# r1 and u of a chunked recurrence as products of 128 rows and 80 columns, decay trees on other engines, and 38 unread products

## The chip, the core and the metric

One core of a Trainium2 chip. The metric is the device time of one execution in microseconds (us), the median of three runs. TensorE is called PE, VectorE DVE, ScalarE ACT, GpSimd POOL, and SP is the queue of SyncE that issues most DMAs.

## What is computed

An RWKV-7 recurrence over four batches, eight heads and 768 steps, with a state of 40x40 for each head, followed by a layer of eight experts that a hash of the token's id chooses:

```python
for t in range(S):
    y[:, :, t] = np.einsum('bhd,bhde->bhe', rt, state)
    Sa = np.einsum('bhde,bhe->bhd', state, at)
    state_decay = state * wt[:, :, None, :] - np.einsum('bhd,bhe->bhde', Sa, bt)
    state = state_decay + np.einsum('bhd,bhe->bhde', vt, kt)
...
expert_idx = token_ids * np.int64(2654435761) % np.int64(E)
...
    h = np.maximum(xe @ w1[e], 0.0)
    out[mask] = h @ w2[e]
```

The experts have D = 320 and F = 1024, there are 3072 tokens, and everything is fp32.

## The kernel before

**Tiles.** The sequence is cut into chunks of 64 steps. A tile is one chunk of two batches (128 rows, all eight heads), so there are 24 tiles, numbered u = 0 to 23; even and odd ones belong to the two pairs of batches. Within a chunk the recurrence is a triangular system. Its right side is r = A·state + (masked A·k)·v, its solution is u. The inverse is built on DVE for four tiles at once (`group_i`: a transpose `nb`, 31 elimination steps on `ub`, two transposes `ut` and `ug`) and completed on PE as `x` and `um`.

**Decays.** `decays(ri)` serves four tiles: from w it makes a tree `lv` of products over 32 rows, then a tree `p` and a tree `q`, and DVE transposes them to `pt` and `qt`, which multiply a and b into `at` and `be` on POOL (DVE for the first `be`). `p` and `q` share one buffer, and both go to DRAM and come back as `py` and `ql`.

**Order.** Every step is entered in a list with a tick, and the sorted list is the order on PE, DVE, ACT and POOL. Each engine runs its instructions in that order. Tile u has its main tick at u + 8. In a tick PE runs: `r0` (state's share of r, 128 rows by 80 columns), `r1` (share of v), `y0` and `y1` (outputs of the tile before), `u`, `ab`, `um`, `tu`, `sd`, `kv`, `s`, `rc`, `rt`, `ak`, `x` and the transposes `at_t`, `bt`. ACT moves r from PSUM as `rhs`, once a tick, so those copies mark the ticks in a trace; they stand at 73.37 for tile 0 and 412 us or so for tile 22. The experts follow from about 431 us on. SP issues the loads in one order too, and each load that needs a buffer back waits there, with all that is queued behind it.

**r1 and u** are each 16 products of 64 rows, 64 columns of weights and 40 columns of data, in an order (`banked`) that puts four beside one another in the array's quadrants. An fp32 product is two records in the trace, so r1 is 32 records and u is 32. Buffers that hold zeros between heads are cleared once at the start by POOL (L135).

Of the kernel before, what the change touches and what calls it, by code (L numbers as in the profile page):

```python
# [42 lines left out]
def kernel(  # L43
# [113 lines left out]

    z_r = ring("z", 3, [ZW], z_gaps)
    r_r = ring("r", 2, [1, H * C], pair_gaps)
    x_r = ring("x", 3, [2, H * C], pair_gaps)  # L160
# [112 lines left out]
    @at_tick(6.08, order=9)  # L273
# [35 lines left out]
    def decays(ri, times, t_out):  # L309
# [36 lines left out]
        for i in range(4, -1, -1):  # L346
            @step
            def _(i=i):
# [3 lines left out]
                eng = nc.gpsimd if ri in (2,) else nc.vector  # L352
# [10 lines left out]
        for i in range(4, -1, -1):  # L363
            @step
            def _(i=i):
                src = x["w"][:] if i == 0 else lv(i)
                d = 1 << i
                if i == 4:
                    x["q"] = spare(ri) if ri < 2 else early.tile([P, BLK, D], F32, tag="pq", name="q")
                    (nc.vector if ri in () else nc.gpsimd).tensor_copy(x["q"][:, BLK - 1], x["ends"][:])  # L370
                q = x["q"]
                eng = nc.vector if ri in () else nc.gpsimd
# [41 lines left out]
    def turned(x, tick, step, src, dst, bufs, by=lambda hp: ident[:]):  # L414
# [18 lines left out]
    def stage_a(u):  # L433
# [4 lines left out]
        if u < 3 * GRP:  # L438
            m = 4.45 + 0.37 * (u - GRP) if u < 2 * GRP else 10.3 + 0.2 * (u - 2 * GRP)
            return m, m + 0.29, m + 0.37  # L440
        return u - 1.4 + (1.0 if u == 3 * GRP else -0.1 if u == 3 * GRP + 1 else 0), None, None

    def tile_a(u):
# [15 lines left out]
        def _():  # L459
# [6 lines left out]
            eng = nc.vector if u < 2 else nc.gpsimd  # L466
# [18 lines left out]
        else:  # L485
            turned(x, u - 1, "at", lambda hp: x["at"][:, hp, :], "at_t", LAG + 2, turning)
# [4 lines left out]
        def _():  # L491
            x["ab_ps"] = p = psum("ab_ps")
            for hp in range(HP):
                for blk in range(2):
                    for par in range(2):
                        for hf in range(2):
                            t0 = blk * BLK
                            r0 = kept(hp, hf) * C + (BLK - t0 if swapped(hp) else t0)
                            o = p[r0:r0 + BLK, par, hp * C:(hp + 1) * C]
                            lhs = x["bt"][half(par), hp, hf, t0:t0 + BLK]  # L500
                            rhs = x["at_t"][half(par), hp, hf, :]
                            if swapped(hp):

                                rhs = bass.AP(rhs.tensor, rhs.offset + BLK, [rhs.ap[0], (-BLK, 2), (1, BLK)])
                            else:
                                rhs = rhs.rearrange("p (two t) -> p two t", two=2)
                            if blk:
                                rhs = rhs[:, 1].unsqueeze(1).to_broadcast([C, 2, BLK])
                            mm(o.rearrange("p (two t) -> p two t", two=2), lhs, rhs)

        @(at_tick(u, "ab", after=0.0) if t_ab is None else at_tick(t_ab + 0.01))
        def _():
# [4 lines left out]
            nc.scalar.copy(groups[gi]["ab"][:, ti].rearrange("p (two h) t -> p two (h t)", two=2), p[:, :, 0:HP * C])  # L517
# [53 lines left out]
    if 0:  # L571
        warm(7.78 - 0.01, 0, gate=True)
    for t_, n_ in ():
        warm(t_, n_)

    def tile_m(u, t0):
# [10 lines left out]
        @(at_tick(t0 - 2, "x") if u > 1 else at_tick(7.78 + 0.02 * u))  # L587
# [10 lines left out]
        @(at_tick(t0 - 2, "x", after=0.0) if u > 1 else at_tick(7.78 + 0.01 + 0.02 * u))  # L598
# [11 lines left out]
        @(at_tick(t0 - 1, "um") if u else at_tick(7.78 + 0.04))  # L610
# [8 lines left out]
        @(at_tick(t0 - 1, "um", after=0.0) if u else at_tick(7.78 + 0.05))  # L619
# [8 lines left out]
    def tile_s(u, t0):  # L628
# [15 lines left out]
        def _():  # L644
            x["r"], x["x"] = r_r(u), x_r(u)
# [6 lines left out]
        def _():  # L652
            load(lambda hf, rows: x["r"][rows, 0].rearrange("t (h x) -> t h x", x=C)[:, :, 0:D], r, n, g)
# [6 lines left out]
        @(at_tick(t0 - 1.41, order=6) if u != 1 else at_tick(8.21))  # L660
# [6 lines left out]
        @(at_tick(t0 - 1.41 + (0.16 if u > 3 else 0.0), order=6) if u != 1 else at_tick(8.21))  # L667
# [40 lines left out]
        turned(x, t0 - 1, "rt", lambda hp: x["r"][:, 0, hp * P:hp * P + R], "r_t", 3)  # L708
# [7 lines left out]
    def tile_b(u, t0):  # L716
# [15 lines left out]
        def _():  # L732
            x["r_ps"] = p = psum("r_ps")
            if n:
                for i in range(HQ):
                    for hf in range(2):
                        for bk in range(2):
                            hp = bk * HQ + i
                            mm(p[half(kept(hp, hf)), bk, i * 2 * D:(i + 1) * 2 * D], x["at_t"][0:R, hp, hf, :],
                               heads(st[0:R, hf ^ j, hp, :]), start=i == 0, stop=False)  # L740

        def own(p, s_, hp, par):
            c0 = (hp % HQ * 2 + par) * D
            return p[half(s_), hp // HQ, c0:c0 + D]
# [12 lines left out]

        @at_tick(t0, "u")
        def _():
            x["u_ps"] = p = psum("u_ps")  # L760
            for hp, hf, par in banked():
                s_ = half(kept(hp, hf))
                mm(own(p, hf, hp, par), x["um"][s_, hx(par, hp), :], x["rhs"][s_, of_head(hp, par)])

        @at_tick(t0, "u", after=0.0)
        def _():
            p = x.pop("u_ps")
            for hf in range(2):
                nc.scalar.copy(x["x"][half(hf), hf].rearrange("t (two h x) -> t two h x", two=2, x=C)[:, :, :, 0:D],
                               p[half(hf), :, 0:HQ * 2 * D].rearrange("t two (h x) -> t two h x", x=D))  # L770
# [654 lines left out]
```

## Time and profile before

| | us |
|---|---|
| median of three runs (684.29 to 688.72) | 684.83 |
| profiled execution, device time | 686.91 |
| its span | 685.1 |
| outside the span | 1.81 |
| ticks of the recurrence, first `rhs` to the last | 73 to 422 |
| experts | 431 to 685 |

PE is busy for 85% of the span. The timeline gives each run of equal instructions with its start, its length, and in brackets how long the engine stood idle before it and whom it waited for. The view by stretches gives busy times with the granted clock of PE (1.00 is the higher of its two levels, 0.50 the lower).

### The profile page before, as it was taken

What the parts mean: (1) busy time and instruction counts of PE and PEld (TensorE: products, weight loads), DVE (VectorE), ACT (ScalarE), POOL (GpSimd) and SP (SyncE); (2) the same over time, 40 slices, a digit from 0 to 9 for tenths busy, and PEclk for the clock granted to TensorE, in tenths of its full rate; (3) what the DMA queues carried; (4) which work ended last, traced back from release to release, by engine and by line L of the source; (5) the groups of instructions that cost most, each with busy time, mean ns of one, the idle gap of its engine ahead of it and who ended that gap; (6) DMA issues with size and microseconds to landing.
All of it is one profiled execution on the core that took longest, in us unless ns stands there. A gap on an engine that the chain in (4) does not pass through costs nothing.

```text
span 685.1 us, 25689 instructions
## 1 busy us (share of the span) xinstructions
PE 584.3 (85%) x11337; PEld 451.4 (66%) x11337; DVE 354.4 (52%) x728; ACT 228.2 (33%) x518; POOL 261.4 (38%) x373
## 2 busy tenths in 40 slices
PE   0444888788979888988879899989999999999994
PEld 0333877677868777877768787867656656565662
DVE  8979998387847695663885761211313131311100
ACT  0233444435645456556444444011111111111110
POOL 6344456455653466444434443222113031211111
PEclk9976667769999899999998999999999999999998
DMA  4566666556556657655677742117646535151000
GB/s 109 134 169 123 131 134 165 113 152 139 110 120 172 131 102 187 127 116 120 149 178 185 192 84 53 41 38 240 189 143 213 172 110 163 47 172 39 29 11 23
DMA packets 184873, 86.07 MB, mean 126 GB/s; under 512 B 159066, under 2 KB 176499, under 8 KB 184756
## 3 DMA queue, kind: packets, MB, share of 16 engines
q1 hardware_dynamic: 177972, 71.54, 42.9%
q0 software_dynamic: 6528, 12.17, 5.9%
q8 instruction: 90, 1.47, 0.9%
q10 hardware_dynamic: 256, 0.66, 0.3%
q14 instruction: 27, 0.22, 0.1%
HBM read 68.51 MB, written 16.11 MB: 124 GB/s over the span
## 4 chain that ended last, share of the span: by engine, by line
PE 60%; DVE 11%; issue 8%; POOL 7%; DMA 6%; SPq 3%; ACT 3%; POOLq 0%; DVEq 0%; ACTq 0%
PE up_ps L233 16%; PE dn_ps L233 12%; PE y_ps L233 4%; PE r_ps L233 3%; PE sd_ps L870 3%; SPq L291 3%; PE rc_ps L233 3%; PE s_ps L233 3%; DVE ub L548 2%; DVE outer L546 2%; PE ue_ps L233 2%; PE kv_ps L431 2%; DVE qt L357 2%; DMA bl<-in_b_dram 2%; PE u_ps L233 1%
## 5 line engine op out<-in xcount | busy, mean ns | idle before, releaser
L233 PE MATMUL up_ps<-xt,w 128*128 128x416 f32 (+3 forms) x384 | 110.1, 498 | 1.3 <-DVE xt L1256 1.3
L233 PE MATMUL dn_ps<-w,ht 128*128 128x320 f32 x352 | 97.2, 432 | 0.0
L233 PEld LDWEIGHTS up_ps<-xt,w 128*128 128x128 f32 (+1 forms) x384 | 58.3, 188 | 51.2 <-issue 45.7
L233 PEld LDWEIGHTS dn_ps<-w,ht 128*128 128x128 f32 x352 | 66.3, 190 | 27.6 <-issue 1.1
L1206 DVE TENSOR_SCALAR ht<-up_ps 128x416 f32<-128x416 f32 (+1 forms) x32 | 17.9, 558 | 106.5 <-PE up_ps L233 106.5
L548 DVE TENSOR_TENSOR ub<-ub,outer 128x60 f32<-128x60 f32 (+9 forms) x180 | 63.8, 354 | 6.2
L546 DVE TENSOR_TENSOR outer<-ub,nb 128x60 f32<-128x60 f32 (+9 forms) x180 | 61.5, 342 | 4.2
L1162 POOL DMA_INDIRECT out_dram<-o,tabs x24 | 23.8, 991 | 91.8 <-ACT o L1212 91.8
L855 POOL TENSOR_TENSOR ys<-ys,py 128x320 f32<-128x320 f32 x24 | 20.7, 862 | 73.0 <-ACT ys L850 73.0
L1208 ACT ACTIVATE ht<-up_ps 128x416 f32<-128x416 f32 (+1 forms) x32 | 15.7, 491 | 86.5 <-PE up_ps L233 86.5
L1212 ACT COPY o<-dn_ps 128x320 f32<-128x320 f32 x22 | 9.4, 426 | 99.4 <-PE dn_ps L233 90.4
L1192 DVE COPY xt<-xg_ps 128x384 f32<-128x384 f32 x22 | 11.0, 551 | 58.5 <-PE xg_ps L1191 58.5
L665 POOL TENSOR_TENSOR z<-kb,ql 128x320 f32<-128x320 f32 x24 | 20.8, 868 | 51.7 <-DMA ql<-q_rows 29.0
L799 DVE TENSOR_TENSOR mr<-rc_ps,after_s 128x1024 f32<-128x1024 f32 x24 | 29.3, 1219 | 15.7 <-PE rc_ps L233 15.7
L233 PE MATMUL rc_ps<-r_t,vu 64*64 64x64 f32 x1536 | 31.3, 234 | 2.1 <-issue 1.3
L1291 POOL COPY htq<-ht 128x256 f32<-128x256 f32 x8 | 3.1, 394 | 77.8 <-DVE ht L1206 67.8
L233 PE MATMUL ab_ps<-at_t,bt 64*32 64x64 f32 x1536 | 23.8, 237 | 10.6 <-ACT at_t L484 5.5
L480 PE MATMUL ab_t_ps<-ident,be 128*128 128x128 f32 x48 | 11.5, 380 | 23.5 <-POOL be L467 12.9
L233 PE MATMUL s_ps<-x,z 128*64 128x40 f32 x704 | 30.6, 252 | 0.7 <-issue 0.7
L870 PE MATMUL sd_ps<-ident,st 128*128 128x128 f32 x176 | 29.8, 319 | 1.2 <-issue 1.1
L607 POOL TENSOR_SCALAR um<-ug,first 128x128 f32<-128x128 f32 x48 | 28.4, 597 | 6.3 <-DVE ug L559 6.3
L233 PEld LDWEIGHTS rc_ps<-r_t,vu 64*64 64x64 f32 x1536 | 27.5, 146 | 4.1 <-issue 2.2
(233 smaller groups left out, 1162.6 us busy)
## 6 DMA issues: line engine op xcount, KB each, us to landing
w<-in_moe_w_dram SPq DMA_DIRECT2D x8, 1280.0 KB
w<-in_moe_w_dram SPq DMA_DIRECT2D x8, 1024.0 KB
ql<-q_rows SPq DMA_DIRECT2D x48, 160.0 KB
al<-in_a_dram SPq DMA_DIRECT2D x48, 80.0 KB
bl<-in_b_dram SPq DMA_DIRECT2D x48, 80.0 KB
p_rows<-pt SPq DMA_DIRECT2D x6, 640.0 KB
q_rows<-qt SPq DMA_DIRECT2D x6, 640.0 KB
kb<-in_b_dram SPq DMA_DIRECT2D x48, 80.0 KB
```

The lines of the kernel that those rows point to most:

```text
L233: nc.tensor.matmul(out_, lhsT=lhsT, rhs=rhs, start=start, stop=stop, skip_group_check=True)
L291: nc.sync.dma_start(dst(hf, half(1 - hf if crossed else hf)), src[batch(g, hf, n % 2), :, n * C:(n + 1) * C, :].rearrange("h t e -> t h e"))
L546: nc.vector.tensor_tensor(tv, ub[:, 0:j + 1, j:j + 1].to_broadcast([P, j + 1, m]), nb[:, j, j + 1:].unsqueeze(1).to_broadcast([P, j + 1, m ...
L548: nc.vector.tensor_tensor(o, o, tv, op=OP.add)
L607: nc.gpsimd.tensor_scalar(um[:, i::2, 0:BLK], groups[gi]["ug"][:, ti * H + i:(ti + 1) * H:2, :], first[:, i:i + 1], None, op0=OP.mult)
L665: nc.gpsimd.tensor_tensor(heads(zv), pairs(x["kb"][:, hf]), pairs(x["ql"][:, hf]), op=OP.mult)
L799: nc.vector.tensor_tensor(t[:].rearrange("p two f h t -> p (two f h) t"), x.pop("rc_ps")[:].rearrange("p two (h t) -> p (two h) t", t=C), ...
L855: nc.gpsimd.tensor_tensor(ys[:], ys[:], x["py"][:], op=OP.mult)
L870: nc.tensor.transpose(p[0:R, f, hp * R:(hp + 1) * R], st[0:R, f, hp, :], ident[0:R, 0:R])
L1162: st = nc.gpsimd.indirect_dma_start(out=out[:], out_offset=bass.IndirectOffsetOnAxis(ap=idx, axis=0), in_=o, in_offset=None, bounds_check= ...
L1206: nc.vector.tensor_scalar(ht[:, f, c:end], ps_[f][:], 0.0, None, op0=OP.max)
L1208: nc.scalar.activation(ht[:, f, c:end], ps_[f][:], AF.Relu)
```

## The change

**r1 and u** become eight products each, of 128 rows, 64 columns of weights and 80 columns of data (two heads side by side, written to two places of the output by a stride): 16 records for 32, two beside one another. One half of each operand is zero: `rhs` becomes one buffer of 128x640 that is cleared once, ACT writes its two halves with two copies (64x320 each) where one of 128x320 was, and the half of `x` that u overwrites is cleared again in every tick on POOL (two clearings of 64x320, after the copies of `um` and ahead of `ys`). At the start POOL clears six more pieces of 64x512 and one of 128x640.

**Decay trees.** `lv` of ri = 2 and `p` of ri = 3, 4 and 5 go from DVE to POOL, `q` of ri = 3 from POOL to DVE, and `be` of tile 1 from DVE to POOL. Many ticks shift by 0.01 to 0.2.

**Unread products.** `warm` puts 38 products of 128x128 with 256 columns into PSUM where nobody reads them: ten ahead of the first x, the others in the next five ticks. One more of two columns reads `go`, which DVE writes near the end of the first elimination (62.65 us before).

```diff
-    x_r = ring("x", 3, [2, H * C], pair_gaps)
+    x_r = ring("x", 3, [2, H * C], lambda t: pair_gaps(t) + [t[half(i), i] for i in range(2)])
+    rhs_r = ring("rhs", 1, [HP, 2, 2, D], lambda t: [t])
...
-                (nc.gpsimd if ri in () else nc.vector).tensor_tensor(lv(i), src[:, 0::2], src[:, 1::2], op=OP.mult)
+                (nc.gpsimd if ri in (2,) else nc.vector).tensor_tensor(lv(i), src[:, 0::2], src[:, 1::2], op=OP.mult)
...
-                eng = nc.gpsimd if ri in (2,) else nc.vector
+                eng = nc.gpsimd if ri in (2, 3, 4, 5) else nc.vector
...
-                eng = nc.vector if ri in () else nc.gpsimd
+                eng = nc.vector if ri in (3,) else nc.gpsimd
...
-            eng = nc.vector if u < 2 else nc.gpsimd
+            eng = nc.vector if u < 1 else nc.gpsimd
...
-    if 0:
-        warm(7.78 - 0.01, 0, gate=True)
-    for t_, n_ in ():
+    if 10:
+        warm(7.77 - 0.01, 10, gate=True)
+    for t_, n_ in ([7.97, 3], [8.21, 2], [8.66, 1], [9.02, 4], [9.33, 5], [9.8, 2], [10.34, 4], [10.55, 2], [11.54, 4], [12.08, 1]):
         warm(t_, n_)
...
-            for hp, hf, par in banked():
-                mm(own(p, kept(hp, hf), hp, par), x["mk"][half(1 - hf), par, hp, :],
-                   x["x"][half(1 - hf), hf, wide(hp, par)], start=n == 0 and hp % HQ == 0 and par == 0)
+            for i in range(HQ):
+                for par in range(2):
+                    for s_ in range(2):
+                        hp, other = HQ * s_ + i, HQ * (1 - s_) + i
+                        at0, at1 = wide(hp, par).start, H * C + wide(other, par).start
+                        mm(both(p[half(s_)], (i * 2 + par) * D, HP * D), x["mk"][:, par, hp, :],
+                           both(x["x"].rearrange("p f c -> p (f c)"), at0, at1 - at0),
+                           start=n == 0 and i == 0 and par == 0)
...
-            nc.scalar.copy(rhs[:].rearrange("p (two x) -> p two x", two=2), x.pop("r_ps")[:, :, 0:HQ * 2 * D])
+            for s_ in range(2):
+
+                o = rhs[half(s_)]
+                o = bass.AP(o.tensor, o.offset + s_ * D, [o.ap[0], (HP * 2 * D + D - 2 * D * s_, 2), (2 * D, HP), (1, D)])
+                nc.scalar.copy(o, p[half(s_), 0:HP * 2 * D].rearrange("p (f h e) -> p f h e", f=2, e=D))
...
-            for hp, hf, par in banked():
-                s_ = half(kept(hp, hf))
-                mm(own(p, hf, hp, par), x["um"][s_, hx(par, hp), :], x["rhs"][s_, of_head(hp, par)])
+            for i in range(HQ):
+                for par in range(2):
                     for hf in range(2):
+                        mm(both(p[half(hf)], (i * 2 + par) * D, HP * D), x["um"][:, hx(par, hf * HQ + i), :],
+                           x["rhs"][:, hf * HQ + i, par].rearrange("p two e -> p (two e)"))
...
+            @at_tick(t0 + 1.2, order=7)
+            def _():
+                for hf in range(2):
+                    nc.gpsimd.memset(x["x"][half(hf), hf].rearrange("t (h x) -> t h x", x=C)[:, :, 0:D], 0.0)
```

**Where instructions move.** On PE, from the last step ahead of the first inverse (`r_t` of tile 0) to u of tile 0, before:

```order
L420 MATMUL r_t_ps<-ident,r_97 128x128 x4
L233 MATMUL x_ps<-ut,abg 64x32 x16
L233 MATMUL ak_ps<-at_t,k_t 64x64 x16
L233 MATMUL x_ps<-ut,abg 64x32 x16
L233 MATMUL um_ps<-ug,xi_110 64x32 x16
L233 MATMUL r_ps<-x_99,mk 64x40 x16
L233 MATMUL u_ps<-rhs,um 64x40 x16
```

and in the change (`idle_ps` is the place nobody reads, `eye` a constant):

```order
L422 MATMUL r_t_ps<-ident,r_97 128x128 x4
L235 MATMUL idle_ps<-go,ident 128x2
L235 MATMUL idle_ps<-eye,ident 128x256 x10
L235 MATMUL x_ps<-ut,abg 64x32 x32
L235 MATMUL ak_ps<-at_t,k_t 64x64 x16
L235 MATMUL um_ps<-ug,xi_111 64x32 x16
L235 MATMUL idle_ps<-eye,ident 128x256 x3
L235 MATMUL r_ps<-x_99,mk 64x2x40 x8
L235 MATMUL idle_ps<-eye,ident 128x256 x2
L235 MATMUL u_ps<-rhs0_102,um 64x2x40 x8
```

Fifteen unread products come ahead of the first u, both x stand ahead of `ak`, and r1 and u have half as many products.

On SP, the loads in the ticks of tiles 2 and 3 (`al` and `bl` are a and b of the tiles 10 to 13, `kb` and `ql` belong to `z` of tile 4, `w` to the decays of ri = 4), before:

```order
L658 DMA py<-p_rows 128x320
L291 DMA al<-in_a_dram 64x8x40 x2
L291 DMA bl<-in_b_dram 64x8x40
L291 DMA kb<-in_b_dram 64x8x40 x2
L291 DMA kb<-in_k_dram 64x8x40 x2
L641 DMA ql<-q_rows 64x2x320 x2
L291 DMA bl<-in_b_dram 64x8x40
L291 DMA al<-in_a_dram 64x8x40 x2
L291 DMA bl<-in_b_dram 64x8x40 x2
L291 DMA x_101<-in_v_dram 64x8x40 x2
L307 DMA w<-in_w_dram 8x1280 x16
L291 DMA al<-in_a_dram 64x8x40 x2
```

and in the change:

```order
L293 DMA al<-in_a_dram 64x8x40 x2
L293 DMA bl<-in_b_dram 64x8x40 x2
L672 DMA py<-p_rows 128x320
L293 DMA kb<-in_b_dram 64x8x40 x2
L293 DMA kb<-in_k_dram 64x8x40 x2
L654 DMA ql<-q_rows 64x2x320 x2
L293 DMA al<-in_a_dram 64x8x40 x2
L293 DMA bl<-in_b_dram 64x8x40 x2
L293 DMA x_101<-in_v_dram 64x8x40 x2
L293 DMA al<-in_a_dram 64x8x40 x2
L293 DMA bl<-in_b_dram 64x8x40 x2
L309 DMA w<-in_w_dram 8x1280 x16
```

The second half of `bl` of tile 11 no longer stands behind `kb` and `ql`, and `al` and `bl` of tile 13 stand ahead of the sixteen loads of `w`.

On POOL, the same place, from `be` of tile 11 to `be` of tile 13, before:

```order
L467 TENSOR_TENSOR be_89<-bl,qt 128x8x40
L607 TENSOR_SCALAR um<-ug,first 128x4x32 x2
L370 COPY q<-ends 128x40
L373 TENSOR_TENSOR q<-q,lv 128x40
L373 TENSOR_TENSOR q<-q,lv 128x2x40
L855 TENSOR_TENSOR ys<-ys,py 128x320
L859 DMA x_rows<-ys 64x320
L860 DMA x_rows<-ys 64x320
L373 TENSOR_TENSOR q<-q,lv 128x4x40
L373 TENSOR_TENSOR q<-q,lv 128x8x40
L373 TENSOR_TENSOR q<-q,w 128x16x40
L467 TENSOR_TENSOR be_89<-bl,qt 128x8x40
```

and in the change:

```order
L476 TENSOR_TENSOR be_89<-bl,qt 128x8x40
L355 TENSOR_TENSOR p<-p,lv 128x40
L355 TENSOR_TENSOR p<-p,lv 128x2x40
L620 TENSOR_SCALAR um<-ug,first 128x4x32 x2
L355 TENSOR_TENSOR p<-p,lv 128x4x40
L355 TENSOR_TENSOR p<-p,lv 128x8x40
L355 TENSOR_TENSOR p<-p,w 128x16x40
L862 MEMSET x_101 64x8x40 x2
L895 TENSOR_TENSOR ys<-ys,py 128x320
L899 DMA x_rows<-ys 64x320
L900 DMA x_rows<-ys 64x320
L476 TENSOR_TENSOR be_89<-bl,qt 128x8x40
```

POOL now makes the tree of `p` there, the tree of `q` is on DVE behind `pt`, and the two clearings of `x` stand ahead of `ys`.

## Rows read from the trace of the kernel before

**Rows 1.** The page: shares of the chain that ended last.

```profile
PE 60%; DVE 11%; issue 8%; POOL 7%; DMA 6%; SPq 3%; ACT 3%; POOLq 0%; DVEq 0%; ACTq 0%
```

**Rows 2.** The view by stretches: setup, first four ticks, later ticks, MoE.

```profile
core 0: us, PE busy (x) PEld busy (x) DVE busy (x) ACT busy (x) POOL busy (x), PEclk, DMA share, GB/s
0.00:68.00 68.00, 25.34 (x632) 20.71 (x632) 58.90 (x116) 16.96 (x36) 33.73 (x69) 0.85 0.59 134
68.00:153.00 85.00, 70.62 (x1820) 62.28 (x1822) 65.11 (x127) 35.48 (x82) 43.56 (x60) 0.70 0.62 139
153.00:431.00 278.00, 245.75 (x7821) 215.13 (x7817) 182.81 (x396) 143.80 (x316) 129.82 (x183) 0.95 0.60 134
431.00:685.00 254.00, 242.56 (x1078) 153.33 (x1074) 47.60 (x91) 31.90 (x85) 54.34 (x61) 0.99 0.34 110
```

**Rows 3.** The timeline from the start, DVE and POOL (start, us, engine, line).

```profile
2.32 6.95 DVE L181 COPY shift<-ident 32x32 f32<-32x32 f32 x2
...
7.25 1.79 POOL L135 MEMSET sd<- 128x640 f32 x3
...
10.14 0.82 DVE L328 TENSOR_TENSOR lv<-w 128x640 f32<-128x640 f32 x1
...
11.00 1.36 DVE L328 TENSOR_TENSOR lv<-lv 128x320 f32<-128x320 f32 x4
```

**Rows 4.** Groups of instructions by form: one clearing of 384 elements on POOL.

```profile
L135 POOL MEMSET z<- 128x384 f32 x3 | 1.2, 432 | 0.0
```

**Rows 5.** The timeline round the first tick.

```profile
64.99 1.09 PE L420 MATMUL r_t_ps<-ident,r 128*128 128x128 f32 x4 [0.15 <-DMA r<-in_r_dram]
...
68.29 1.08 PE L233 MATMUL x_ps<-ut,abg 32*64 32x32 f32 x32 [2.20 <-DVE ut L558]
...
71.10 2.16 DVE L532 STREAM_TRANSPOSE nb<-abg 128x1024 f32<-128x1024 f32 x1
...
73.94 1.09 PE L233 MATMUL u_ps<-rhs,um 64*64 64x40 f32 x32 [0.64 <-ACT rhs L756]
```

**Rows 6.** The timeline of the tick that ends at 152.71.

```profile
125.10 0.43 ACT L756 COPY rhs<-r_ps 128x320 f32<-128x320 f32 x1
...
126.10 1.38 SPq L291 DMA_DIRECT2D bl<-in_b_dram  x1
...
129.56 0.86 POOL L467 TENSOR_TENSOR be<-bl,qt 128x320 f32<-128x320 f32 x1 [7.31 <-DMA bl<-in_b_dram]
...
130.40 1.18 POOL L607 TENSOR_SCALAR um<-ug,first 128x128 f32<-128x128 f32 x2
...
130.47 1.12 PE L480 MATMUL ab_t_ps<-ident,be 128*128 128x128 f32 x4 [4.13 <-POOL be L467]
...
139.49 2.70 DVE L357 STREAM_TRANSPOSE qt<-q 128x1280 f32<-128x1280 f32 x1 [13.74 <-POOL q L373]
...
144.13 0.86 POOL L467 TENSOR_TENSOR be<-bl,qt 128x320 f32<-128x320 f32 x1 [4.67 <-DMA bl<-in_b_dram]
...
152.71 0.43 ACT L756 COPY rhs<-r_ps 128x320 f32<-128x320 f32 x1 [0.91 <-PE r_ps L233]
```

**Rows 7.** The timeline of r0, r1, y0 and y1 in a steady tick.

```profile
397.83 0.78 PE L233 MATMUL r_ps<-st,at_t 128*64 128x80 f32 x16
...
398.53 0.68 PE L233 MATMUL r_ps<-x,mk 64*64 64x40 f32 x32
...
399.14 0.77 PE L233 MATMUL y_ps<-sd,r_t 128*64 128x80 f32 x16
...
399.75 0.96 PE L233 MATMUL y_ps<-z,mr 128*64 128x40 f32 x28
```

**Rows 8.** The timeline: a stop of PE inside a run of equal products.

```profile
359.81 0.78 PE L233 MATMUL y_ps<-z,mr 128*64 128x40 f32 x20 [2.16 <-issue]
```

**Rows 9.** The timeline of the MoE: dn, products of 320 columns.

```profile
509.67 8.78 PE L233 MATMUL dn_ps<-w,ht 128*128 128x320 f32 x32
```

**Rows 10.** The timeline: u behind POOL's um in a later tick.

```profile
231.06 0.68 PE L233 MATMUL u_ps<-rhs,um 64*64 64x40 f32 x32 [1.56 <-POOL um L607]
```

More of the change, by code (lines that the diff above doesn't have):

```diff
@@ L156, in z_gaps, with wide_gaps @@
         return [t.rearrange("p (h x) -> p h x", x=C)[:, :, D:C]]
+    def wide_gaps(t):
+        return [t[half(i), :, :, 1 - i, :] for i in range(2)]
     z_r = ring("z", 3, [ZW], z_gaps)
     r_r = ring("r", 2, [1, H * C], pair_gaps)
-    x_r = ring("x", 3, [2, H * C], pair_gaps)
+    x_r = ring("x", 3, [2, H * C], lambda t: pair_gaps(t) + [t[half(i), i] for i in range(2)])
+    rw_r = ring("rw", 1, [HP, 2, 2, C], wide_gaps) if 1 == 2 else lambda u: None
+    aw_r = ring("aw", 1, [HP, 2, 2, C], wide_gaps) if 0 else lambda u: None
+    rhs_r = ring("rhs", 1, [HP, 2, 2, D], lambda t: [t])
     st_r = ring("st", NG, [2, HP, R], lambda t: [t])
@@ L212, in kept, with slot @@
         return hf ^ (hp // HQ)
+    def slot(hp, hf):
+        return hf * HQ + hp % HQ
     def swapped(hp):
@@ L271, in at_tick @@
         return add
-    @at_tick(6.08, order=9)
+    @at_tick(5.9, order=9)
     def _():
@@ L412, in decays, with turned @@
                 at_tick(k0 + w_ * i / len(fs), order=8)(f)
-    def turned(x, tick, step, src, dst, bufs, by=lambda hp: ident[:]):
+    def turned(x, tick, step, src, dst, bufs, by=lambda hp: ident[:], wide_r=None):
         @at_tick(tick, step)
@@ L424, in _ @@
             x[dst] = t = work.tile([P, HP, 2, C], F32, tag=dst, name=dst, bufs=bufs)
-            nc.scalar.copy(t[0:R].rearrange("p h f t -> p (h f t)"), x.pop("ps_" + dst)[0:R])
+            p = x.pop("ps_" + dst)
+            nc.scalar.copy(t[0:R].rearrange("p h f t -> p (h f t)"), p[0:R])
+            if wide_r is not None:
+                x[dst + "w"] = tw = wide_r
+                for par in range(2):
+                    rows = half(par)
+                    nc.scalar.copy(tw[rows, :, :, par, :].rearrange("p h f t -> p (h f) t"),
+                                   p[rows].rearrange("p (h t) -> p h t", t=C))
     def turned_rows(p, c0, src):
@@ L491, in _ @@
         def _():
-            x["ab_ps"] = p = psum("ab_ps")
+            by_pair = "at_tw" in x
+            p = psum1("ab_ps") if by_pair else psum("ab_ps")
+            x["ab_ps"] = p = (p.rearrange("p (h two t) -> p two h t", two=2, t=C) if by_pair else
+                              p[:, :, 0:HP * C].rearrange("p two (h t) -> p two h t", t=C))
             for hp in range(HP):
                 for blk in range(2):
-                    for par in range(2):
+                    for par in range(1 if by_pair else 2):
                         for hf in range(2):
@@ L516, in _ @@
             groups[gi]["tiles"] = ti + 1
-            nc.scalar.copy(groups[gi]["ab"][:, ti].rearrange("p (two h) t -> p two (h t)", two=2), p[:, :, 0:HP * C])
+            nc.scalar.copy(groups[gi]["ab"][:, ti].rearrange("p (two h) t -> p two h t", two=2), p)
     def group_i(gi, t0, t1, t2):
@@ L732, in _, with both @@
         def _():
-            x["r_ps"] = p = psum("r_ps")
+            x["r_ps"] = p = psum1("r_ps")
             if n:
[L735 to L744, printed above, removed]
+                for i in range(HP):
+                    for s_ in range(2):
+                        hf = i // HQ
+                        hp = i % HQ + HQ * (hf ^ s_)
+                        mm(p[half(s_), i * 2 * D:(i + 1) * 2 * D], x["at_t"][0:R, hp, hf, :],
+                           heads(st[0:R, hf ^ j, hp, :]), start=i == 0, stop=False)
+        def both(t, first_, step):
+            return bass.AP(t.tensor, t.offset + first_, [t.ap[0], (step, 2), (1, D)])
         @at_tick(t0, "r1")
@@ L768, in _ @@
             for hf in range(2):
-                nc.scalar.copy(x["x"][half(hf), hf].rearrange("t (two h x) -> t two h x", two=2, x=C)[:, :, :, 0:D],
-                               p[half(hf), :, 0:HQ * 2 * D].rearrange("t two (h x) -> t two h x", x=D))
+                nc.scalar.copy(x["x"][half(hf), hf].rearrange("t (h x) -> t h x", x=C)[:, :, 0:D],
+                               p[half(hf), 0:DM].rearrange("t (h x) -> t h x", x=D))
         @at_tick(t0, "tu")
```

98 lines of the change are left out of this document (53 added, 45 removed).

## The prediction

> **What bounds the kernel now.** I read the chain that ended last first, then the busy times by stretches, then the timeline at the places the change touches. The chain gives 60% to PE's own work, 8% to "issue" (PE waits for nothing the profile shows), 11% to DVE, 7% to POOL and 9% to DMA and SP's queue [rows 1]. The stretches say where each of these counts [rows 2]. Up to 68 us DVE is busy for 58.9 of 68: the first decays and the first elimination are the bound, and what delays DVE there delays the end. From 68 to 153, the first ticks, PE is busy for 70.6 of 85 and DVE for 65.1, and PE's granted clock is 0.70, so much of that work ran at the lower of its two levels: u of tile 0 took 1.09 [rows 5], where a group of as many and as large records takes 0.68 later [rows 7]. From 153 to 431 PE is busy for 88% at a clock of 0.95. From 431 on the experts fill PE at 0.99, and the change has nothing there. So 431 us are in play.
>
> **The change part by part**, against the profiled execution of 686.91 (span 685.1 and 1.81 around it), which is 2.08 above the median of 684.83.
>
> *Start.* At 2.32 DVE starts two copies of 32x32 that take 6.95 us and end 0.2 us behind the last of POOL's clearings (7.25 + 1.79 = 9.04); only then does the tree `lv` begin [rows 3]. So DVE stood until POOL's whole run of clearings was over. The change adds six of 512 elements and one of 640 to that run. 384 elements took 0.43 [rows 4] and 640 took 1.79/3 = 0.60 [rows 3], so 512 is about 0.52, and the seven are 6 x 0.52 + 0.60 = 3.7 us. The ends are 0 (the copies slip in between two clearings) and +3.7; I take **+3.5**, since no gap between clearings let the copy in before. Nothing covers it, for DVE sets the pace up to 68 us.
> The Trainium skill (SBUF - State Buffer, section "Who interferes with whom") says that DVE and GpSimd share a port pair that is an exclusive lock, held for the instruction that got it first. By that rule the copy would wait for the clearing in flight alone, the added ones would cost nothing, and the sum would be 3.5 lower; the row, in which it waited for the run, speaks against this.
>
> *The first ticks.* PE was free at 64.99 + 1.09 = 66.08 and waited 2.20 us for `ut` before the first x at 68.29 [rows 5]. Ten products now stand there. One of `dn`'s records of 320 columns takes 8.78/32 = 0.27 us [rows 9], so 256 columns are 0.22 and a product of two records 0.44 (0.88 at half clock). Ten are 4.4 to 8.8; with the clock rising halfway I take 6.6, so x starts at 72.7, 4.4 late, and `nb`, the next elimination's first step (71.10), as late. Against that stand three gains. The groups behind x run at the higher level: 1.09 - 0.68 = 0.41 for each of some eight up to 78 us, -3.3. DVE loses `lv` of ri = 2, as large as the tree of [rows 3], 0.82 + 1.36 = 2.2 us. And if the granted clock from 68 to 153 goes from 0.70 to 0.85, PE's 70.6 us shrink by 70.6 x (1 - 0.70/0.85) = 12.5, which pays for the other 28 products (12.3). What is left is the delay of DVE, 4.4 - 2.2, and five products (2.2) ahead of the first u, less 3.3 and some: **+0.5**, from -3 (the clock gains more than the products cost) to +5 (the delay passes through and the clock gains nothing ahead of DVE).
>
> *The tick from 125.10 to 152.71.* It lasts 27.6 us, and three waits make it long [rows 6]. `be` of tile 11 waited 7.31 on POOL for a half of `bl` that SP issued only at 126.10, because `kb` stood ahead of it and waits for a `z`; behind that `be` stand `um` (130.40) and, on PE, a transpose that waited 4.13. DVE waited 13.74 for POOL's tree `q` before `qt` at 139.49. And `be` of tile 13 waited 4.67 for a `bl` queued behind the sixteen loads of `w`. The new order on SP puts both loads ahead, which takes away PE's 4.13 and POOL's 4.67: 8.8. The tree `q` on DVE falls in the 13.74 it spent idle. What is late next is `um`: two steps of the tree `p`, now on POOL, stand ahead of it. Best case: a tick of 14.6, -13. Worst: `p` on POOL takes the place of the wait, -2. I take **-8**, near the two waits' sum.
>
> *Records.* Per tick r1 and u lose 16 records each. r0 has the new shape already, 16 records of 128x64 and 80 columns: it holds PE for 398.53 - 397.83 = 0.70 behind x, and y0, of the same shape, for 0.61; r1 in its old form takes 0.61 too [rows 7]. So the new form costs 0.61 to 0.70 where the rows follow a group of another shape. The 0.09 between the two I read as a price of changing shapes. In the change r0, r1, y0, y1 and u all have 64 columns of weights and 128 rows, so r1, y0 and u no longer follow another shape. I put 0.54 on each, an estimate: -0.07 for each of three groups, -0.2 per tick, over 22 ticks **-4.5**. If nothing is saved by equal shapes it is 0; if each of the two costs r0's 0.70, 2 x 0.09 x 22 = +4; if twice the estimate is saved, -7 after what is hidden.
> The Trainium skill speaks against this part: TensorE: Matmul & The Clock Gate, Part 3 (packing small matmuls), has tiles of the array run beside one another at a few ns more for each, so that four quadrants of 40 columns beat two halves of 80. By it r1 and u would cost more than 0.61 each and the term would be at its end of +4. y0's 0.61 with 80 columns doesn't bear that out.
>
> *Clock later.* At 0.95 over 278 us [rows 2] a tenth, 27.8 us, ran at the lower level and cost up to 13.9. The low stretches lie where PE had waited or its groups had few rows; records of 128 rows in place of 64 may keep some of them up. I take **-2.5**, from -6 (somewhat under half of the 13.9) to +2 (PE does less and falls more).
>
> *Instruction supply.* PE stopped for 2.16 in the middle of y1, waiting for nothing shown [rows 8], one of thirteen such stops. The change drops 768 of the 10273 matmul records ahead of the experts (7.5%) and as many weight loads: **-1** (0 to -1.5).
>
> *POOL and ACT.* Two clearings of 64x320 a tick cost POOL about 0.4 each, by [rows 4], so 19 us in all; POOL is busy for 130 of 278 us [rows 2], which hides nearly all. Where u waits for POOL's `um`, as with 1.56 in one tick [rows 10], POOL's lateness passes through: **+1.5** (0 to +3). The second copy of `rhs` on ACT (0.43) lies beside y0 and y1, which stand between r1 and u on PE; without that cover it would be 24 x 0.43 = 10.
>
> The sum: 3.5 + 0.5 - 8 - 4.5 - 2.5 - 1 + 1.5 = -10.5. 686.91 - 10.5 = 676.4 profiled, and 2.08 less as a median: **674**.
>
> **The rivals.**
> *The early gain is eaten* (about no change). Start +3.7, first ticks +4 because `nb` is as late as x and DVE is the bound there, the long tick -6, equal shapes worth -1, clock -2, supply -1, POOL +1.5: -0.8, so 684. For it speaks that DVE has little slack up to about 100 us; against it the 2.2 that DVE sheds.
> *The clock stays low under the unread products* (slower than before). If the granted clock does not rise during the first ten, all 38 take 0.88, 33.4 us. The holes of PE from 68 to 153 are 85 - 70.6 = 14.4, and 2.2 ahead of x; if half of these 16.6 lies where the products stand, some 25 us come on top of the path in place of +0.5: the sum is +14, 698. It decides at a clock of about 0.6 over that stretch: with half of the products at the high level the surplus is 13 and the time 687. Against it: the array has full rows and columns in them, as in `dn`, which ran at 0.99.
> *Wide records hold the clock* through the later ticks: the clock term becomes -10 and the time 666. For it: PE is busy in 88% of that stretch already. Against it: the stops for instructions remain.
> *The long tick keeps its length*, since `p` on POOL holds up `um`, and `pt` and `q` follow each other on DVE through one shared buffer: -2 there, 680.
>
> **How the numbers follow.** Chances: the forecast 0.47, the eaten gain 0.20, the low clock 0.11, the held clock 0.10, the long tick 0.12. A measurement of this kernel tells about 1%, 6.8 us, from no change: below 678.0 is faster, above 691.7 slower. Faster: 0.42 of the forecast's, all of the held clock's and a third of the long tick's, 0.56. Slower: the low clock and a little of the eaten gain's bad end, 0.12. The rest, 0.32, lies within 1%. The range reaches from 663, the held clock with a good long tick, to 688, the eaten gain's bad end and the low clock's mild form; the forecast's own is 667 to 681.
>
> **What would show it.** Right: the first `lv` on DVE at about 13.6 in place of 10.14; x of tile 0 near 76 (3.5 and 4.4 later), at a granted clock of 1.00 soon behind it; the long tick at 19 to 20 us; r1 and u at 0.5 to 0.6 in steady ticks; the experts unchanged at 254 us. Wrong: `lv` where it was (the start term is 0); a clock of 0.5 from 66 to 78; u waiting for `um` behind `p`; r1 over 0.7; `um` waiting for the clearings of `x` in most ticks.

## The result and the profile after

The change takes 677.18 us (676.40 to 678.17, four runs) against 684.56 (683.53 to 688.72): a ratio of 0.989, 95% interval 0.984 to 0.994, so 7.4 us. The prediction was 674, with a range of 663 to 688. The profiled execution has a span of 676.1, 9.0 below [rows 2]'s 685.

The `rhs` copies mark the ticks. In us from the start:

| `rhs` of tile | before | after | difference |
|---|---|---|---|
| 0 | 73.37 | 73.39 | 0.0 |
| 3 | 125.10 | 123.88 | -1.2 |
| 4 | 152.71 | 142.63 | -10.1 |
| 5 | 166.63 | 157.93 | -8.7 |
| 7 | 199.60 | 195.59 | -4.0 |
| 9 | 230.53 | 225.31 | -5.2 |
| 11 | 262.18 | 262.62 | +0.4 |
| 23 | 422.13 | 413.88 | -8.3 |

So the long tick gains 8.9, the ticks of tiles 5 to 7 and 9 to 11 give back 10.3 (4.7 and 5.6), and from tile 11 on 8.7 come back: at tile 11 the change has gained nothing in this profile, and what the total shows arises behind it. The same stretches of time as in [rows 2], in the changed kernel:

```profile
0.00:68.00 68.00, 31.89 (x652) 26.73 (x653) 56.87 (x116) 16.96 (x36) 41.09 (x80) 0.80 0.63 142
68.00:153.00 85.00, 74.20 (x2028) 62.16 (x2030) 67.09 (x138) 42.82 (x98) 50.88 (x74) 1.00 0.63 144
153.00:431.00 278.00, 245.12 (x6983) 218.01 (x6980) 174.25 (x375) 147.49 (x325) 151.22 (x231) 0.93 0.60 132
431.00:676.00 245.00, 233.40 (x996) 145.63 (x995) 45.85 (x85) 30.87 (x83) 49.59 (x56) 0.99 0.35 112
```

From 68 to 153 PE's granted clock is 1.00 where it was 0.70; later it is 0.93 where it was 0.95. PE is not less busy in these two stretches. The experts take as long as before: 262.2 us from `rhs` of tile 23 to the end of the span, against 263.0.

The start of the changed kernel, against [rows 3]:

```profile
2.33 3.97 DVE L187 COPY shift<-ident 32x32 f32<-32x32 f32 x2
...
4.42 3.44 POOL L135 MEMSET x<- 128x384 f32 x7
...
8.09 0.82 DVE L330 TENSOR_TENSOR lv<-w 128x640 f32<-128x640 f32 x1 [0.66 <-DMA w<-in_w_dram]
```

The two copies of `shift` end after 3.97 us, not 6.95, in the middle of POOL's clearings of `x` (3.44 us for seven), and `lv` begins 2 us earlier, not 3.5 later. It then waits 0.66 for its load of w.

The first x and what stands ahead of it, against [rows 5]:

```profile
62.69 1.92 DVE L571 STREAM_TRANSPOSE ut<-ub 128x1024 f32<-128x1024 f32 x1
...
62.70 6.06 PE L235 MATMUL idle_ps<-eye,ident 128*128 128x256 f32 x20
...
68.69 1.14 PE L235 MATMUL x_ps<-ut,abg 32*64 32x32 f32 x64
...
71.22 2.18 DVE L545 STREAM_TRANSPOSE nb<-abg 128x1024 f32<-128x1024 f32 x1
```

`ut` begins at 62.69, 3.6 us earlier than before, and the ten products (20 records, 6.06 us) end at 68.69. So x starts 0.4 later than before: they used up what the start had gained.

The long tick, against [rows 6]:

```profile
121.30 0.86 POOL L476 TENSOR_TENSOR be<-bl,qt 128x320 f32<-128x320 f32 x1
...
122.81 1.19 POOL L620 TENSOR_SCALAR um<-ug,first 128x128 f32<-128x128 f32 x2
...
127.08 2.73 DVE L359 STREAM_TRANSPOSE pt<-p 128x1280 f32<-128x1280 f32 x1 [8.71 <-POOL p L355]
...
135.79 0.86 POOL L476 TENSOR_TENSOR be<-bl,qt 128x320 f32<-128x320 f32 x1 [5.61 <-PE r_t_ps L422]
...
142.63 0.86 ACT L782 COPY rhs<-r_ps 64x320 f32<-64x320 f32 x2
```

`be` of tile 11 runs at 121.30 without a wait (7.31 before), `um` at 122.81, and the tick ends after 18.75 us in place of 27.61.

One steady tick, against [rows 7]:

```profile
402.83 0.78 PE L235 MATMUL r_ps<-st,at_t 128*64 128x80 f32 x16
...
403.44 0.77 PE L235 MATMUL r_ps<-x,mk 128*64 128x80 f32 x16
...
404.04 0.72 PE L235 MATMUL y_ps<-sd,r_t 128*64 128x80 f32 x16
...
404.59 1.08 PE L235 MATMUL y_ps<-z,mr 128*64 128x40 f32 x32
...
405.49 0.75 PE L235 MATMUL u_ps<-rhs,um 128*64 128x80 f32 x16
...
406.18 0.94 PE L235 MATMUL um_ps<-ug,xi 32*64 32x32 f32 x32
```

From start to start r0 takes 0.61 (0.70 before), r1 0.60, y0 0.55 (0.61), y1 0.90, u 0.69. Medians of such differences over the ticks of tiles 13 to 23, before and after: r0 0.70 and 0.61, r1 0.61 and 0.56, y0 0.60 and 0.55, y1 1.01 and 0.91, u 0.60 and 0.70. The sum falls by 0.19 a tick.

In the ticks that got longer POOL holds the tree of `p`:

```profile
171.14 0.87 POOL L679 TENSOR_TENSOR z<-kb,ql 128x320 f32<-128x320 f32 x1 [8.11 <-DMA r<-in_r_dram]
...
173.60 0.87 POOL L355 TENSOR_TENSOR p<-p,lv 128x320 f32<-128x320 f32 x1
...
174.42 0.73 POOL L853 TENSOR_TENSOR sc<-sc,pend 128x320 f32<-128x320 f32 x1
...
175.18 0.93 ACT L867 COPY st<-sc 64x320 f32<-64x320 f32 x2 [3.74 <-POOL sc L853]
...
175.92 1.54 POOL L355 TENSOR_TENSOR p<-p,w 128x640 f32<-128x640 f32 x1
...
177.49 2.72 DVE L359 STREAM_TRANSPOSE pt<-p 128x1280 f32<-128x1280 f32 x1 [9.44 <-POOL p L355]
```

POOL stands 8.11 us ahead of `z`, which reads the loads `kb` and `ql` (the profile names `r`, issued behind them), and the last two of the five steps of `p` come behind it. `sc`, the new state, stands behind one of them on POOL's queue, ACT's `st` waits 3.74 for it, and `pt` waits 9.44 for the end of `p`.

### The profile page after: what moved, and what is told of

Same layout as the page of the kernel before. It is cut to its first block, busy times and chain, and to the rows that moved or that the text cites. A ratio compares the mean times of both kernels' runs of the same rounds, so it can differ in the third digit from the quotient of the medians.

```text
span 676.1 us, 24439 instructions
## 1 busy us (share of the span) xinstructions
PE 584.6 (86%) x10647; PEld 452.5 (67%) x10647; DVE 344.1 (51%) x713; ACT 238.1 (35%) x542; POOL 292.8 (43%) x439
## 4 chain that ended last, share of the span: by engine, by line
PE 61%; DMA 9%; POOL 8%; issue 8%; DVE 6%; SPq 5%; ACT 3%; POOLq 0%; DVEq 0%; ACTq 0%
PE up_ps L235 16%; PE dn_ps L235 12%; SPq L293 4%; PE y_ps L235 4%; PE r_ps L235 3%; PE sd_ps L910 3%; DMA al<-in_a_dram 2%; PE rc_ps L235 2%; DMA ql<-q_rows 2%; PE s_ps L235 2%; PE u_ps L235 2%; PE ue_ps L235 2%; DMA w<-in_w_dram 2%; PE kv_ps L440 2%; PE ab_ps L235 2%
## 5 line engine op out<-in xcount | busy, mean ns | idle before, releaser
L235 PE MATMUL y_ps<-z,mr 128*64 128x40 f32 x768 | 28.0, 234 | 1.7 <-issue 1.1
L235 PE MATMUL ak_ps<-at_t,k_t 64*64 64x64 f32 x768 | 17.6, 225 | 13.8 <-DVE sc L852 10.0
L235 PE MATMUL rc_ps<-r_t,vu 64*64 64x64 f32 x1536 | 28.5, 224 | 0.7 <-ACT vu L807 0.7
L359 DVE STREAM_TRANSPOSE pt<-p 128x1280 f32<-128x1280 f32 x6 | 16.3, 2712 | 24.8 <-POOL p L355 24.6
L476 POOL TENSOR_TENSOR be<-bl,qt 128x320 f32<-128x320 f32 x23 | 20.7, 899 | 18.9 <-PE r_t_ps L422 5.6
```

The source lines that it names most:

```text
L235: nc.tensor.matmul(out_, lhsT=lhsT, rhs=rhs, start=start, stop=stop, skip_group_check=True)
L476: eng.tensor_tensor(heads(x["be"][:]), pairs(x["bl"][:]), decay(rounds[ri]["qt"]), op=OP.mult)
```

## The experiments

All ratios are to the kernel before on the same chip, whose median was 684 to 686 there with a spread of some 15 us, so a ratio is uncertain by 0.4 to 0.7%; the ticks and waits of the profiles tell more than the totals. The changed kernel itself has 0.989.

**Without the unread products** (`e1_no_unread`).

```diff
-    if 10:
+    if 0:
...
-    for t_, n_ in ([7.97, 3], [8.21, 2], [8.66, 1], [9.02, 4], [9.33, 5], [9.8, 2], [10.34, 4], [10.55, 2], [11.54, 4], [12.08, 1]):
+    for t_, n_ in ():
```

> The changed kernel without its unread products. First theory (the gain comes from the long tick, and the unread products only pay for themselves): x of tile 0 starts near 64.7 us in place of 68.7, the granted clock from 68 to 153 falls from 1.00 to about 0.7, the two cancel, and the time is 677 give or take 3. Rival (the clock that they hold up is the gain): about 686, no faster than the kernel before.

Measured: 0.992 (0.988 to 0.996). x starts at 64.19, the tick of tile 2 is 15.49 in place of 13.91 and the long tick 20.78 in place of 18.75. The first theory holds: x is 4.5 us earlier than in the change and `rhs` of tile 4, at 142.80, 0.2 later. The clock did not fall to 0.7 but to 0.87 over that stretch. The first tick kept its length, 11.50 to 11.48. In the change:

```profile
76.97 1.15 PE L235 MATMUL s_ps<-x,z 128*64 128x40 f32 x32
...
81.34 0.68 DVE L719 TENSOR_TENSOR mk<-ak_ps,after_s 128x512 f32<-128x512 f32 x1
...
82.07 1.99 PE L235 MATMUL idle_ps<-eye,ident 128*128 128x256 f32 x8 [0.22 <-DVE mk L719]
...
84.00 0.78 PE L235 MATMUL r_ps<-x,mk 128*64 128x80 f32 x16
```

Without the unread products:

```profile
74.22 1.95 PE L235 MATMUL s_ps<-x,z 128*64 128x40 f32 x32
...
80.14 0.77 PE L235 MATMUL r_ps<-x,mk 128*64 128x80 f32 x16 [0.48 <-DVE mk L719]
```

Without them `s` takes 1.95 where it takes 1.15 at the high level, and r1 of tile 1 waits for DVE's `mk` alone. With them `mk` is ready at 82.02, and r1 starts 2 us later, behind four unread products. What the clock gives in this tick, the products take.

**The unread products alone** on the kernel before (`e5_only_unread`).

> The kernel before with the 38 unread products and the one of two columns alone. First theory: x of tile 0 starts four us late, the clock from 68 to 153 rises to 0.9 or more and gives back about as much, 683 to 687. Rival (the clock is the gain): 678.

Measured: 1.005 (1.000 to 1.010); nearer to the first theory, which falls short in the delay and in the clock (0.86 from 68 to 153):

```profile
67.89 6.67 PE L233 MATMUL idle_ps<-eye,ident 128*128 128x256 f32 x20
...
74.49 0.67 PE L233 MATMUL x_ps<-ut,abg 32*64 32x32 f32 x32
...
79.01 0.43 ACT L756 COPY rhs<-r_ps 128x320 f32<-128x320 f32 x1 [0.97 <-PE r_ps L233]
```

x starts 6.2 us late and tile 0 stands 5.6 behind [rows 5]'s kernel; tile 20 is at 388.65, against 387.69. Without an earlier start they cost 5.6 us at tile 0, and in the total between nothing and 1%.

**r0, r1 and u in their old form** within the change (`e3_narrow`).

```diff
-                        mm(both(p[half(s_)], (i * 2 + par) * D, HP * D), x["mk"][:, par, hp, :],
...
+                mm(own(p, kept(hp, hf), hp, par), x["mk"][half(1 - hf), par, hp, :],
+                   x["x"][half(1 - hf), hf, wide(hp, par)], start=n == 0 and hp % HQ == 0 and par == 0)
...
-                    nc.gpsimd.memset(x["x"][half(hf), hf].rearrange("t (h x) -> t h x", x=C)[:, :, 0:D], 0.0)
```

> The changed kernel with r0, r1 and u in their old form: 64 rows and 40 columns in four quadrants, one rhs copy, no clearings of x and rhs. First theory (equal shapes save 0.2 us a tick and the clearings cost 1.5 in all): slower than the change by 3, so 680. Rival (four quadrants are as good, and the clearings on POOL, the second copy and the seven clearings at the start cost): faster than the change, about 673.

Measured: 1.002 (0.997 to 1.007), some 9 us above the change, three times what the first theory gave and far from the rival. The copies of `shift` take 6.95 us again and `lv` begins at 10.13, so the early start belongs to the wide form, by its clearings. But the start explains little of the surplus: x is only 1.7 us later than in the change, since the unread products ate the gain there, and `rhs` of tile 11, at 261.88, is 0.7 ahead of the change. The surplus arises behind it: from there to `rhs` of tile 23 this kernel takes 163.0 us and the change 151.3. (r0 has the same shape in both; only the order and the place of its products go back.)

**The wide form alone** on the kernel before (`e4_only_wide`; `r_t` has two buffers, as in the change, to make room).

> The kernel before with r0, r1, u, rhs and the clearings in the changed form alone (decay trees, loads and ticks as before, no unread products). First theory (the clearings of 64 rows start DVE's chain 3.6 us earlier, the records save 0.19 us a tick): faster by 3.6 + 4.2 less what the clearings on POOL cost, so 6 to 8 us, a ratio of 0.989 to 0.991, with the long tick still near 27 us. Rival (the gain of the change is its long tick, the wide form gives 3 at most): 0.995 or more.

Measured: 0.990 (0.983 to 0.996), the first theory: 7 us with a long tick of 26.87. From `rhs` of tile 11 to that of tile 23 it takes 153.0 us, where the kernel before takes 160.0.

**Six clearings more at the start, and nothing else**, of 64 rows (`e6_clear64`, the first + line) or of 128 (`e7_clear128`, the second). No one reads what they clear; the work is that of the kernel before.

```diff
-    x_r = ring("x", 3, [2, H * C], pair_gaps)
+    x_r = ring("x", 3, [2, H * C], lambda t: pair_gaps(t) + [t[half(i), i] for i in range(2)])
+    x_r = ring("x", 3, [2, H * C], lambda t: pair_gaps(t) + [t[:, i] for i in range(2)])
```

> The kernel before with six more clearings of 64 rows by 512 elements among POOL's clearings at the start, and nothing else. First theory (DVE's two copies get in during clearings of 64 rows): the copies end near 6.3 in place of 9.3, the first lv is at 8.1 to 8.4, the transposes ut start some 3.6 us earlier, and the time falls by about 3.5. Rival (as the prediction had it, the copies wait for the whole run, and something else in the change let them in): lv near 13, slower by 3.

> The kernel before with the same six pieces cleared over all 128 rows at the same place. First theory (128 rows keep the copies out until the run ends): lv at about 10.1 + 6 x 0.5 = 13.2, the time 3 us longer. Rival (what counts is the number or the order of the clearings, not their rows): lv near 8.2 as in the kernel with 64 rows.

Measured: 0.9925 (0.989 to 0.996) with 64 rows, 1.003 (0.998 to 1.008) with 128. With 64 rows:

```profile
2.32 3.94 DVE L181 COPY shift<-ident 32x32 f32<-32x32 f32 x2
...
4.41 3.40 POOL L135 MEMSET x<- 128x384 f32 x7
...
8.06 0.82 DVE L328 TENSOR_TENSOR lv<-w 128x640 f32<-128x640 f32 x1 [0.68 <-DMA w<-in_w_dram]
...
8.64 1.09 POOL L135 MEMSET x<- 64x512 f32 x2
...
11.99 1.36 DVE L353 TENSOR_TENSOR p<-p,lv 128x40 f32<-128x40 f32 x4
...
12.69 2.87 POOL L373 TENSOR_TENSOR spare<-spare,lv 128x40 f32<-128x40 f32 x4
...
13.39 0.86 DVE L353 TENSOR_TENSOR p<-p,w 128x640 f32<-128x640 f32 x1
```

With 128:

```profile
2.32 9.73 DVE L181 COPY shift<-ident 32x32 f32<-32x32 f32 x2
...
4.41 2.99 POOL L135 MEMSET x<- 128x384 f32 x7
...
8.22 1.00 POOL L135 MEMSET x<- 128x512 f32 x2
...
12.93 0.82 DVE L328 TENSOR_TENSOR lv<-w 128x640 f32<-128x640 f32 x1
```

The tree `p` in the kernel before:

```profile
13.76 2.25 POOL L373 TENSOR_TENSOR spare<-spare,lv 128x40 f32<-128x40 f32 x4
...
14.06 2.29 DVE L353 TENSOR_TENSOR p<-p,lv 128x40 f32<-128x40 f32 x4
...
16.39 2.04 DVE L353 TENSOR_TENSOR p<-p,w 128x640 f32<-128x640 f32 x1
```

The same count of clearings at the same place: 128 rows hold the two copies for 9.73 us, 64 rows let them in after 3.94. The trace shows where they get in. Two clearings of 64x512 take 1.09 us, more than twice the 0.52 of one: 0.04 to 0.05 us are free between them, and the first copy ends at 5.69, in the first such gap. Two of 128x512 take 1.00, less than twice the 0.54 of one: each begins before the one ahead has ended, and there is no gap. On the start both theories are confirmed: the prediction's price holds for clearings of 128 rows, lv at 12.93, and fails for those that the change makes. On the time the one for 128 rows is not: x of tile 0 is 1.8 us later, at 70.07, not 2.8, and the total can't be told from the kernel before.

There is a second gain. The tree `p` follows at 11.99 and takes 1.36 + 0.86 = 2.2 us; before, it took 2.29 + 2.04 = 4.3. Before, POOL's tree `q` (`spare`) had begun 0.3 us ahead of it, at 13.76. With 64 rows `p` begins 0.7 ahead, and its last steps run beside POOL's first ones at full speed; there POOL's four steps take 2.87, against 2.25 before. x starts at 64.64, 3.65 earlier.

**p of ri = 4 and 5 back on DVE** (`e2_p45_dve`).

```diff
-                eng = nc.gpsimd if ri in (2, 3, 4, 5) else nc.vector
+                eng = nc.gpsimd if ri in (2, 3) else nc.vector
```

> The changed kernel with the trees p of ri = 4 and 5 back on DVE. First theory (these trees on POOL made the ticks from 158 to 197 and from 225 to 263 long, by some 10 us against the kernel before): those ticks shrink and the time is 668 to 672. Rival (the ticks are long because the granted clock fell there, 0.74 and 0.77, for lack of work in the records of 128 rows): the clock and the ticks stay, 677.

Measured: 0.986 (0.980 to 0.993), 672.13. The four ticks ending at tiles 6, 7, 10 and 11 take 16.64, 14.89, 15.02 and 17.46, together 64.0, where the change takes 75.0 and the kernel before 64.6:

```profile
173.57 2.70 DVE L359 STREAM_TRANSPOSE pt<-p 128x1280 f32<-128x1280 f32 x1
...
176.32 0.93 ACT L867 COPY st<-sc 64x320 f32<-64x320 f32 x2
...
178.12 0.86 ACT L782 COPY rhs<-r_ps 64x320 f32<-64x320 f32 x2 [0.88 <-PE r_ps L235]
```

`pt` and `st` wait for nobody there. The granted clock of 153 to 431 is 0.95 again: in the change's order the trees lengthened these ticks, and the clock followed. The total's gain over the change (0.3%) lies within the intervals.

**The trees of ri = 3 back** (`e9_tree3_back`: `p` on DVE, `q` on POOL) **and the loads back** (`e10_loads_back`, whose edit this is).

```diff
-            m = 4.54 + 0.37 * (u - GRP) if u < 2 * GRP else 10.3 + 0.18 * (u - 2 * GRP)
+            m = 4.54 + 0.37 * (u - GRP) if u < 2 * GRP else 10.3 + 0.2 * (u - 2 * GRP)
...
-        @at_tick(ri * 4 - 5.07 if ri > 3 else (-4, -2.9, 4.22, 10.04)[ri], order=9)
+        @at_tick(ri * 4 - 5.12 if ri > 3 else (-4, -2.9, 4.22, 10.04)[ri], order=9)
```

> The changed kernel with the trees of ri = 3 as before: p on DVE and q on POOL; loads and ticks stay changed. First theory (the order of the loads makes the long tick shorter, the trees little): the tick of tile 3 to 4 stays at 19 to 22 us in place of 18.8, the time within 2 us of the change. Rival (the tree q on DVE is what shortens it): 24 or more, the time 5 us above the change.

> The changed kernel with two ticks as before, so that on SP the second half of bl of tile 11 stands behind kb and ql again, and a and b of tile 13 behind the sixteen loads of w; the trees stay changed. First theory (the loads make the long tick): be of tile 11 waits 6 us or more for bl again, the tick is 25 to 27, the time 5 to 8 us above the change. Rival (the trees): the tick stays under 21 and the time with it.

Measured: 0.989 (0.983 to 0.995) with the trees back, a long tick of 20.17; 0.998 (0.993 to 1.003) with the loads back, and 28.84:

```profile
126.53 0.60 SPq L293 DMA_DIRECT2D bl<-in_b_dram  x1
...
129.89 0.86 POOL L476 TENSOR_TENSOR be<-bl,qt 128x320 f32<-128x320 f32 x1 [6.77 <-DMA al<-in_a_dram]
...
135.32 2.73 DVE L359 STREAM_TRANSPOSE pt<-p 128x1280 f32<-128x1280 f32 x1 [15.74 <-POOL p L355]
...
152.91 0.86 ACT L782 COPY rhs<-r_ps 64x320 f32<-64x320 f32 x2 [0.94 <-PE r_ps L235]
```

With the second half of `bl` at 126.53 again, `be` waits 6.77, and the tick is as long as before. Two numbers, of 0.02 and 0.05 of a tick, hold the long tick's gain; the trees change it by 1.4 us.

Both kernels also say something of the trees `p` of ri = 4 and 5, which stay on POOL in them. The ticks to tiles 6 and 7 together take 30.3 us with the trees of ri = 3 back and 30.8 with the loads back, against 37.7 in the change and 33.0 before, and `z` no longer waits there (`z` at 166.60 and 171.12). So the first tree costs its 5 us only where POOL's queue also stands before that load. `e11_p45_none`, below, has `p` on DVE and such a wait of 7.99, and takes 34.1: some 3 us go with the wait and some 3.5 with the tree behind it, an estimate from single profiles. The ticks to tiles 10 and 11 stay long, 36.3 and 37.0 (37.3 in the change, 31.7 before). And in the profile of the kernel with the loads back, `rhs` of tile 11 is at 262.43, 0.2 ahead of the change: all that the long tick had lost is made up by then. The totals, 0.998 and 0.989, still differ by 6 us, with intervals that just overlap.

**p of 4 and 5 on DVE, with fewer unread products**: 28 (`e8_p45_28`) or none (`e11_p45_none`).

> The changed kernel with the trees p of ri = 4 and 5 on DVE and without the first ten unread products; the other 28 stay. First theory (the ten cost 4 us ahead of the first x and give back less than that): x of tile 0 near 64.5, the time 2 to 4 us below the kernel with p of 4 and 5 on DVE alone, 668 to 670. Rival (without them the clock stays low until far into the first ticks, which costs as much): the same 672 or more.

> The changed kernel with p of ri = 4 and 5 on DVE and without any unread product: what the other experiments point to. First theory (the unread products pay for themselves and no more): 672 give or take 2, the same as with them. Rival (they gain through the clock): 676 or more; third (they cost): 669 or less.

Measured: 0.987 (0.983 to 0.992), 675.82, and 0.984 (0.980 to 0.989), 672.23. With 28 x starts at 64.26, but `rhs` of tile 0 gains only 3 us against all 38, since the others then run at the low level and wait themselves; nothing is won, as the rival had it. With none the time is that of all 38 (672.13): the first theory. The last has the lowest ratio here, 11 us (1.6%) below the kernel before; its lead over the change, 0.5%, lies within the intervals.

## Why the prediction was right, term by term

The total was off by 3 us and its direction was right, but that is luck in part: two terms failed by 7 to 9 us each and cancelled. By place the forecast has +4 up to tile 3, where -1.2 was measured; -8 for the long tick (-8.9); and -6.5 behind it, where the next seven ticks gave back 10.5 and the last twelve brought 8.7. Of its own signs the long tick, the clock of 1.00 and r1 came as said; `lv` (8.09), x (68.69) and u (0.70) did not.

*Start, +3.5: measured -3.65, the sign wrong.* The step that failed is "no gap between clearings let the copy in before". That was so of clearings of 128 rows; the added ones have 64 rows, no row of the trace before showed one, they leave gaps, and the copies get in there (`e6_clear64` against `e7_clear128`). The stated lower end of 0 excluded a gain without a reason. "Nothing covers it" was wrong too: in `e7_clear128` 2.8 us at `lv` were 1.8 at x. The lock of one instruction that the Trainium skill has (SBUF - State Buffer, "Who interferes with whom") did not let a copy in after the clearing in flight: with 128 rows it waited through the run, 9.73 us, and got in only where POOL's row has a gap. What the Trainium skill says in the same section of DVE instructions with two inputs in SBUF, that they contend with GpSimd's reads, agrees with the tree `p`: 4.3 us where POOL's tree had begun first, 2.2 where it had not, and there POOL's steps took longer.

*First ticks, +0.5: about +2.* Between the kernel with the 64-row clearings alone and the change, x moves from 64.64 to 68.69 and `rhs` of tile 3 from 121.81 to 123.88. Against the change without its unread products (122.02) it is 1.9. The ten products were sized right (6.06 us against 6.6; 5.1 to 7.1 in the other profiles). The clock rose to 1.00, more than the 0.85 taken, but gave less: without the products it is 0.87 already (`e1_no_unread`), and the other 28 stand in the path themselves, as r1 of tile 1 shows.

*Long tick, -8: measured -8.9*, by the cause named: `e10_loads_back` restores it, `e9_tree3_back` does not. Whether it would reach the end was not asked: `rhs` of tile 11 is at 262.18 before, 262.62 in the change and 262.43 in `e10_loads_back`.

*Records, -4.5: measured -0.19 a tick, -4.2 over 22*, but not from the groups named. Put were -0.07 each for r1, y0 and u; r1 and y0 gave 0.05 each, r0 and y1 gave 0.09 and 0.10, and u became 0.10 dearer. Measured from start to start, the price for changing shapes stands at the group ahead of the change: r0 and y1 stood ahead of quadrants and no longer do, u now stands ahead of `um`'s. There were two such places and there is one. By the packing rule of the Trainium skill (TensorE: Matmul & The Clock Gate, Part 3) r1 and u would each have cost more than 0.61; r1's 0.56 disagrees at 80 columns, u's 0.70 does not.

*Clock later, -2.5, and instruction supply, -1.* From 153 to 431 us the clock gave nothing: 0.93 in place of 0.95 in the change, 0.95 with `p` back on DVE. The last twelve ticks say more. From `rhs` of tile 11 to that of tile 23 the five kernels here with the old form of r1 and u take 157.4 to 163.0 us, the eight with the new one 151.3 to 154.4, whatever their trees, loads and unread products (one profile each): 7.8 us less in the mean, and the form is what divides them. The records' 0.19 a tick are 2.3 of that. Stops of PE over 0.15 us that wait for nothing shown fall from 13.9 us (13 to 18 stops) to 11.0 (8 to 12), in the pair of before and after from 15.4 to 8.3; so -1 was too small. What is left goes with a clock of 0.97 in the mean in place of 0.94; the two ranges overlap, and its share stays open. Before tile 11 the two forms do not divide the kernels. Together the three terms were put at -8, near the 7.8, and the shares inside came otherwise.

*POOL, +1.5: about +10.* The clearings were priced at 0.4 and took 0.36 each; one wait for them shows in the change, of 0.33 us. What was left out is the tree `p` of ri = 4 and 5: it was named as moved and given no price of its own, though each puts five more steps on the queue on which `sc` and `um` stand (`e2_p45_dve`: 64.0 for 75.0 in four ticks). The 10 us are its price in the change's order; with the loads or the trees of ri = 3 back, the first of the two costs nothing.

The rivals: the low clock under the unread products did not happen (1.00). The eaten gain was half right: the ten products ate the start's gain, only that there was one. The long tick did not keep its length, but `p` on POOL did hold up the state and `pt`, two ticks later than that rival has it.

## What to carry to other kernels

Price each moved instruction by what stands behind it in its new queue, not by the busy share of its new engine: POOL was idle for more than half of the time before, and two trees of five steps cost 10 us, because the state's update and a wait for a load stand in the same queue. An edit's side effects on a shared resource can be as large as the edit: half or more of the wide form's 7 us alone came from clearings that happened to have 64 rows (0.9925 against 0.990), so try the side effect alone. A wait on a load can be an issue order: two numbers in the schedule were worth 10 us of one tick. A gain in one tick is not yet a gain at the end: see where the next ticks put it.

## What the runs showed of the hardware that was not expected

Two DVE copies of 32x32 took 3.94 to 3.98 us where POOL's run of clearings had some of 64 rows, 6.95 where all had 128, and 9.73 when six more of 128 rows were added. They got in where POOL's row leaves 0.04 us between two clearings of 64 rows; why those leave it stays open. DVE's products of 128x640 took 0.82 to 0.86 beside clearings, or beside POOL's products where DVE's tree had begun first, and 2.04 where POOL's had. And products that no one reads held the granted clock at 1.00 for 85 us (0.87 without them), and the time did not fall by it.
